# Feed-forward in pairs, free choice of PSUM banks, weights in ten pieces: a linear-attention and FFN kernel on one core

## The chip, the cores and the metric

The kernel runs on 1 core of one Trainium2 chip. The metric is the device time of one execution in microseconds (us). "Span" is the part of it that the profile covers, about 1 to 2 us less. The engines are TensorE (PE in the profile; its weight loads are PEld), VectorE (DVE), ScalarE (ACT), GpSimd (POOL) and SyncE (SP, which only issues transfers here). Each engine works through its own list of instructions in the order in which the program was built, and waits by semaphores for the others.

## The reference

```python
# B=4, H=8, S=768, D=48; FFN 384 -> 2048 -> 384 over 3072 tokens
for t in range(S):
    cur = einsum('bhd,bhe->bhde', u[None] * kt, vt)
    y[:, :, t] = einsum('bhd,bhde->bhe', rt, state + cur)
    state = w[None, :, :, None] * state + einsum('bhd,bhe->bhde', kt, vt)
x = y.transpose(0, 2, 1, 3).reshape(B * S, H * D)
return maximum(x @ w_in, 0) ** 2 @ w_out
```

The kernel cuts time into 6 chunks of 128 steps. A chunk of one batch is a *unit*; there are 24 of them, and a unit is also one block of 128 rows of the FFN.

## The kernel before

The program lists small operations with their engines, estimated durations and dependencies. A greedy scheduler in Python then puts them in order while the program is built. So the order of every engine is fixed at build time, by modelled times. Per unit: load k, r, v; multiply by powers of w (`kw`, `rw`); `rk`, `rku`, `du`, `dv` for the u term; transposes and attention matmuls on TensorE (`trk`, `trr`, `am`, `ym`, `yt`) with two masks, `sm` and `yb` on DVE in between. The FFN follows for groups of units:

```python
ps_ring("a", 3); ps_ring("h", 3); ps_ring("o", 2)          # fixed shares of the 8 PSUM banks
...
nc.sync.dma_start(out=wb, in_=bass.AP(tensor=w.tensor, offset=w.offset, ap=[[0, 128], [1, HD]]))  # ahead of the first k
...
groups = [[0, 1], [2, 3]] + [list(range(i, i + B)) for i in range(B, NU, B)]   # two pairs, then fours
W_IN_AT, W_OUT_AT = (0, 0, 1, 1), (3, 3, 4, 4)             # w_in in 4 parts at units 0, 0, 1, 1; w_out at 3, 3, 4, 4
...
for us in groups:
    L = len(us)
    for f in range(NF):                                     # 16 blocks of 128 hidden columns
        def m1(e, ...):
            t = ps_tile(h, [128, L * C], F32)               # 512 columns for a four, 256 for a pair
            for kk in range(NK):
                nc.tensor.matmul(out=t, lhsT=w_in_sb[:, kk, f * 128 : (f + 1) * 128], rhs=xt..., ...)
        # relu on DVE or ACT, square on ACT or POOL, both on [128, L * C]
    for j, n in enumerate(us):
        for part in range(PARTS):                           # m2: 4 matmuls of w_out at a time
            ...
```

## Time and profile before

| | before |
|---|---|
| time, median of the first runs | 202.22 us (201.72 to 204.4) |
| span | 201.1 us |
| TensorE, DVE, ACT, POOL busy | 90%, 67%, 64%, 67% |
| first transposes of unit 0 | 9.8 us |
| first FFN matmul | 24.7 us |
| FFN of the first four units done | 64.0 us |
| last weights landed | 52.2 us |
| last matmul started | 197.1 us |

The page's 40 slices (5 us each) of the kernel before show the regimes. A digit is the busy share of that slice in tenths; PEclk is the clock granted to TensorE.

```profile
PE   7474798696699799999999999999999999999992
DVE  5896868279976787896988558887476564555200
POOL 2665918279969999999998999989984010422200
PEclk9976559999999999999999999999999999999999
DMA  4999999947349999848555649210011001111122
```

TensorE is full from slice 14 (70 us; slices are counted from 0) on, and holes fill the time before. The sums by windows of 10 us of the same kernel follow; after the window and its length come PE, PEld, DVE, ACT and POOL busy (number of instructions), the granted clock, the share of the transfer engines and GB/s.

```profile
10.00:20.00 10.00, 6.16 (x62) 3.94 (x61) 7.89 (x12) 3.87 (x6) 6.20 (x7) 0.67 1.10 188
20.00:30.00 10.00, 8.63 (x67) 6.16 (x65) 7.20 (x15) 5.11 (x11) 5.56 (x8) 0.50 1.12 194
50.00:60.00 10.00, 7.96 (x85) 4.92 (x84) 8.85 (x14) 5.08 (x9) 8.29 (x8) 1.00 0.39 77
```

Busy PE includes matmuls on zeros that are only meant to keep its clock up ("fillers"), so busy is not work. The chain of waits of the kernel before, in order of time (start, length, what), names the holes:

```profile
9.18 8.82 DMA rt<-in_r_dram
...
30.70 8.73 DMA w_out_sb<-in_moe_w_out_dram
...
50.29 1.27 DVE rp_74 L256
...
62.14 0.96 POOL kp_79 L253
63.09 1.27 POOL rp_76 L256
```

A load beside w_in, then w_out, then DVE and POOL that prepare units 4 to 7 one operation after another. The first group of four cannot start its FFN before all its four units are prepared.

One number is used: *useful work*. It is the sum, over TensorE's matmuls without fillers that started before a time t, of the spacing that each costs at full clock. The spacing is taken from the Trainium skill, "TensorE: Matmul & The Clock Gate", Back-to-back issue gap (columns/2.4 + 2.5 ns for a warm TensorE; the section calls it the gap of an isolated matmul, and gives about 131 ns each for a stream of 512-column ones). The formula holds in rows too: 9 matmuls of 512 columns in 1.94 us before, 216 ns each. The float32 matmuls of the start are left out. In all it is 161.3 us before, and it shows how far TensorE has come at a given time.

### The profile page before, as it was taken

The numbers are of one execution on the slowest core, as the hardware profiler recorded it, in microseconds if no ns is written. First come the engines' busy times: TensorE is split into PE (matmuls) and PEld (weight loads), VectorE is DVE, ScalarE is ACT, GpSimd is POOL, SyncE is SP. The second block draws the span as 40 slices with busy tenths as digits, with TensorE's granted clock in tenths as the row PEclk, the third lists the DMA queues.
The fourth block names the chain that finished last, engine by engine and source line by source line (L and its number), as shares of the span: only waits on it lengthen the run. The fifth ranks groups of instructions, "written<-read, shape, count | busy, mean of one in ns | idle before, by whom it ended". The sixth has DMA issues, their size and how long they took to land.

```text
span 201.1 us, 4167 instructions
## 1 busy us (share of the span) xinstructions
PE 180.6 (90%) x1565; PEld 108.8 (54%) x1565; DVE 134.0 (67%) x239; ACT 128.7 (64%) x243; POOL 135.2 (67%) x155
## 2 busy tenths in 40 slices
PE   7474798696699799999999999999999999999992
PEld 2143476474356446565565665566556655555551
DVE  5896868279976787896988558887476564555200
ACT  3533458468366488899978979876687755444211
POOL 2665918279969999999998999989984010422200
PEclk9976559999999999999999999999999999999999
DMA  4999999947349999848555649210011001111122
GB/s 108 199 173 204 181 209 131 209 81 110 50 105 255 210 179 213 176 86 199 119 117 118 158 83 203 73 39 18 26 42 39 35 7 39 41 39 42 39 78 78
DMA packets 82368, 22.68 MB, mean 113 GB/s; under 512 B 75436, under 2 KB 82348, under 8 KB 82348
## 3 DMA queue, kind: packets, MB, share of 16 engines
q1 hardware_dynamic: 78480, 19.08, 43.6%
q0 software_dynamic: 3712, 3.15, 10.3%
q10 hardware_dynamic: 156, 0.20, 0.4%
q8 instruction: 12, 0.20, 0.4%
q14 instruction: 8, 0.07, 0.1%
HBM read 20.84 MB, written 4.72 MB: 127 GB/s over the span
## 4 chain that ended last, share of the span: by engine, by line
PE 70%; DMA 9%; DVE 7%; POOL 5%; SPq 4%; issue 2%; ACT 1%; POOLq 0%; DVEq 0%; ACTq 0%
PE ps_h L396 28%; PE ps_o L429 28%; DMA rt<-in_r_dram 4%; PE ps_a L274 4%; DMA w_out_sb<-in_moe_w_out_dram 4%; SPq L241 4%; PE ps_a L321 3%; PE ps_a L364 2%; PE ps_a L346 2%; PE ps_a L341 2%; DVE AT L331 2%; PE ps_a L291 1%; POOL rk L247 1%; DVE rku L250 1%; POOL rku L250 1%
## 5 line engine op out<-in xcount | busy, mean ns | idle before, releaser
L407 DVE TENSOR_SCALAR gr<-ps_h 128x512 f32<-128x512 f32 (+1 forms) x84 | 51.7, 624 | 35.8 <-PE ps_h L396 30.9
L396 PEld LDWEIGHTS <-w_in_sb 128*128 128x128 bf16 x336 | 31.6, 100 | 20.6 <-issue 0.6
L331 DVE TENSOR_TENSOR AT<-ps_a,smask 128x512 bf16<-128x512 f32 x48 | 30.8, 682 | 3.8 <-PE ps_a L321 3.7
L247 POOL TENSOR_TENSOR rk<-rt,kt 128x384 f32<-128x384 f32 x24 | 25.4, 1062 | 6.0 <-DVE wsq L203 3.9
L280 ACT COPY rkT<-ps_a 128x1024 bf16<-128x1024 bf16 x24 | 24.3, 1011 | 4.7 <-PE ps_a L274 4.5
L250 POOL TENSOR_TENSOR rku<-rk,ub 128x384 f32<-128x384 f32 x20 | 20.2, 1008 | 0.3
L264 POOL TENSOR_TENSOR dv<-vb,du 128x384 f32<-128x384 bf16 x21 | 17.6, 840 | 3.9 <-DVE du L261 3.0
L409 ACT ACTIVATE gr<-ps_h 128x512 f32<-128x512 f32 (+1 forms) x28 | 13.8, 502 | 9.6 <-PE ps_h L396 9.2
L416 POOL TENSOR_TENSOR g_2869<-gr 128x512 bf16<-128x512 f32 x5 | 5.2, 1039 | 20.6 <-DVE gr L407 20.6
L437 ACT COPY osb<-ps_o 128x384 f32<-128x384 f32 x24 | 11.4, 476 | 11.3 <-PE ps_o L429 11.3
L259 ACT CAST vb<-vt 128x384 bf16<-128x384 f32 x24 | 12.1, 509 | 7.7 <-DMA vt<-in_v_dram 7.7
L354 DVE TENSOR_TENSOR yb<-ps_a,dv 128x384 bf16<-128x384 f32 x24 | 13.2, 550 | 4.6 <-PE ps_a L346 4.5
L261 DVE TENSOR_REDUCE du<-rku 128x8 f32<-128x384 f32 x24 | 13.1, 544 | 1.8 <-POOL rku L250 1.5
L149 PE MATMUL ps_a<-zb 128*128 128x512 bf16 (+1 forms) x28 | 10.6, 503 | 2.8 <-DVE zb L144 1.3
L429 PE MATMUL ps_o<-w_out_sb,g_2038 128*128 128x384 bf16 x64 | 13.0, 326 | 0.0
L429 PE MATMUL ps_o<-w_out_sb,g_1578 128*128 128x384 bf16 x64 | 12.9, 326 | 0.0
L429 PE MATMUL ps_o<-w_out_sb,g_2501 128*128 128x384 bf16 x64 | 12.9, 326 | 0.0
L396 PE MATMUL ps_h<-xt_2120,w_in_sb 128*128 128x512 bf16 x48 | 12.8, 379 | 0.0
L396 PE MATMUL ps_h<-xt_2624,w_in_sb 128*128 128x512 bf16 x48 | 12.8, 379 | 0.0
L429 PE MATMUL ps_o<-w_out_sb,g_1150 128*128 128x384 bf16 x64 | 12.7, 326 | 0.0
L396 PE MATMUL ps_h<-xt_1681,w_in_sb 128*128 128x512 bf16 x48 | 12.7, 379 | 0.0
L414 ACT ACTIVATE g_2501<-gr 128x512 bf16<-128x512 f32 x15 | 9.5, 633 | 4.8 <-DVE gr L407 4.6
(182 smaller groups left out, 394.5 us busy)
## 6 DMA issues: line engine op xcount, KB each, us to landing
kt<-in_k_dram SPq DMA_DIRECT2D x24, 192.0 KB, 3.6
rt<-in_r_dram SPq DMA_DIRECT2D x24, 192.0 KB, 4.1
vt<-in_v_dram SPq DMA_DIRECT2D x24, 192.0 KB, 4.0
out_dram<-osb SPq DMA_DIRECT2D x24, 192.0 KB, 2.1
w_in_sb<-in_moe_w_in_dram POOLq DMA_DIRECT2D x4, 384.0 KB, 7.7
w_out_sb<-in_moe_w_out_dram POOLq DMA_DIRECT2D x4, 384.0 KB, 6.0
wb<-in_w_dram SPq DMA_DIRECT2D x1, 192.0 KB, 3.8
ub<-in_u_dram ACTq DMA_DIRECT2D x1, 192.0 KB, 3.9
```

The source lines that it names most:

```text
L247: two(lambda e, T=T: e.tensor_tensor(T("rk"), T("rt"), T("kt"), ALU.mult)),
L250: two(lambda e, T=T: e.tensor_tensor(T("rku"), T("rk"), ub, ALU.mult)),
L259: lambda e, T=T: nc.scalar.copy(T("vb"), T("vt")), takes=[bufs["vb"]], uses=[bufs["vt"]])
L261: lambda e, T=T: nc.vector.tensor_reduce(T("du"), T("rku"), axis=mybir.AxisListType.X, op=ALU.add),
L264: two(lambda e, T=T: e.tensor_tensor(T("dv"), T("vb"), T("du")[:, :, None].to_broadcast([C, H, D]), ALU.mult)),
L280: lambda e, T=T, rk_p=rk_p: nc.scalar.copy(T("rkT"), rk_p.tile),
L331: lambda e, T=T, i=i, x=x: nc.vector.tensor_tensor(T("AT")[:, i], x.tile, smask[:, None, :].to_broadcast([128, NP, C]), ALU.mult),
L354: lambda e, T=T, y_p=y_p: nc.vector.tensor_tensor(T("yb"), y_p.tile.rearrange("t p i d -> t (p i d)"), T("dv").rearrange("t h d -> t (h d) ...
L396: nc.tensor.matmul(out=t, lhsT=w_in_sb[:, kk, f * 128 : (f + 1) * 128], rhs=xt.tile[:, kk].rearrange("p b t -> p (b t)"), start=(kk == 0), ...
L407: nc.vector.tensor_scalar(gr.tile[:, : L * C], h.tile, 0.0, None, ALU.max)
L409: nc.scalar.activation(gr.tile[:, : L * C], h.tile, AF.Relu)
L429: nc.tensor.matmul(out=o_p.tile, lhsT=g.tile[:, f, j, :], rhs=w_out_sb[:, f, :], start=(f == 0), stop=(f == NF - 1),)
```

## The change

Its intent is to let FFN start sooner and to fill the first 70 us:

```diff
-    groups = [[0, 1], [2, 3]] + [list(range(i, i + B)) for i in range(B, NU, B)]
+    for j in range(NU // L):                       # L = 2: pairs throughout
+        us = [units[L * j], units[L * j + 1]]
...
+        for f in range(NH):                        # NH = 8; two row blocks of h in one bank
+            def m1(...):
+                for z in range(2):
+                    for kk in range(NK):
+                        nc.tensor.matmul(out=psv(h, 2, L * C)[:, z],
+                            lhsT=w_in_sb[:, kk, (2 * f + z) * 128 : (2 * f + z + 1) * 128], ...)
...
-    ps_ring("a", 3); ps_ring("h", 3); ps_ring("o", 2)
+    limits = {"a": 4, "h": 3, "o": 4}              # any free bank, up to a limit per use
...
-    W_IN_AT, W_OUT_AT = (0, 0, 1, 1), (3, 3, 4, 4)
+    PIECES = (0, 1, 2, 4, 6, 8)                    # five pieces of w_in, five of w_out, in turn
+    w_ops.append(weights(i, which, w_ops[-3] if len(w_ops) >= 3 else units[2]["vt"]))
+    load(n, nm, w_ops[-3] if n == 4 and nm == "kt" else None)   # unit 4's k waits for weights
...
-    nc.sync.dma_start(out=wb, ...)                 # w over 128 partitions, 192 KB; u likewise
+    nc.tensor.matmul(out=psv(wb_p, H, D), lhsT=ones, rhs=wrow[:, :, :D], ...)   # float32, from 1.5 KB
+    nc.tensor.matmul(out=psv(ub_p, HD), lhsT=ones, rhs=urow, ...)
```

Further: six buffers for loads instead of five, three for x and g, `rkT`, `xt` and `osb` copies on ACT or DVE, DVE's help for the first six units instead of eight, measured durations in the scheduler's model, w^128 by Ln and Exp instead of seven squarings.

## The prediction

> What bounds it now. In the page's slices TensorE is full from 70 us to 197 us, with holes before. Start to start in the timeline, at full clock: three 128x512 matmuls of w_in take 0.65 us, four 128x384 of w_out 0.65 us, one unit's attention about 1.5 us. A unit (24 in all) costs 5.2 + 1.5 = 6.7 us, all together 161 us (estimate from these). The span is 201.1: some 36 us are start, holes and low clock (0.67 and 0.50 in 10 to 30 us), 3.6 us follow the last matmul.
>
> The holes, by the chain of waits up to 75 us: no transposes until 9.8 us (wb, 192 KB, before the first k; two table loads; seven squarings of wc); 9.2 to 18.0 an r load competing with w_in; 30.7 to 39.4 w_out; 42 to 69 DVE and POOL preparing four units while TensorE has little FFN. At 70 us four units' FFN is done.
>
> What changes. (1) Pairs throughout: xt of two units releases FFN, so most of the third hole (units 4 to 7) goes. w_in matmuls are 256 wide and double in number. The trace has some: nine to twelve in a row take 0.110 to 0.117 us each, against 0.108 for half of a 512-wide one; the change costs 1 to 4 us. The Trainium skill, "TensorE: Matmul & The Clock Gate", Back-to-back issue gap, gives N/2.4 + 2.5 ns, 109 ns, which agrees. Relu and square stay 128x512 (0.62, 0.63 us), so DVE, ACT and POOL work per unit hardly changes (about 16.6 of 20.2 us). (2) Free bank choice: 1 to 3 us of PSUM waits. (3) wb and ub (384 KB) become 3 KB and float32 matmuls; one activation table: transposes at about 7 instead of 9.8 us. (4) Weights wait for unit 2's v, three pieces in flight; unit 4's k waits for weights. Transfers stay the limit at first: DMA share is 1.1 in 10 to 40 us. By the queue table k, r, v cost about 3.2 us per unit, all weights 20.7 us of sixteen engines (estimates from its shares). "DMA: Bandwidth & Descriptors", Specifications, names 512 B as minimum for line rate; 75,436 of 82,368 packets are smaller, which stays. Four units, the weights and parts of two more divided by 1.1 give 37 us: FFN of pairs 0 and 1 runs as pieces land, from about 17 us, ending about 41; pair 2 starts about 45, after a small hole.
>
> Sum: from 45 us remain 20 units' FFN (104 to 107 us), 18 units' attention (27), the last chain (1 to 2) and 3.6: span 181, time about 182 us. Range 175 to 192. Faster by over 2%: 0.94; within 2%: 0.05; slower: 0.01.
>
> What would show it: real transposes near 7 us; w_in's first FFN matmul before 20 us (24.7 now); last weights landing at 35 to 43 us; TensorE tenths of 9 from slice 9 or 10; four units' FFN done by 45 us; 256-wide w_in matmuls spaced 0.109 to 0.117 us; POOL no longer at 100%.
>
> What would make it wrong: an instruction order made for weights that land sooner than they do, TensorE standing behind a piece with other work ready; low clock to 40 us, as fillers end early; DVE or ACT late for attention; POOL and DVE slowing one another (DVE multiplications of 0.55 us take up to 1.35).

## The result

| | before | after |
|---|---|---|
| time, median | 201.97 us (201.5 to 204.4, 4 runs) | 191.87 us (190.73 to 193.31, 4 runs) |
| ratio to before | | 0.951 (0.945 to 0.957) |
| span of the profiled run | 201.1 us | 190.1 us |
| first transposes of unit 0 | 9.8 us | 12.6 us |
| first FFN matmul | 24.7 us | 22.8 us |
| FFN of the first four units done | 64.0 us | 52.5 us |
| last weights landed | 52.2 us | 40.0 us |
| useful work at 30, 45, 70 us | 6.5, 18.2, 34.5 us | 8.1, 22.7, 46.0 us |

Ratios here and below are the mean time of one kernel's fast runs over that of the other's of the same rounds, so not quite the ratio of the medians that are quoted. A later set gave the changed kernel 191.43 us (190.07 to 193.43; one of the six is slow, the fast ones end at 192.2), ratio 0.949 (0.945 to 0.954). Its executions scatter by 2 to 3 us, which matters for what follows.

The gain is 10 us, where 20 were expected. The slices of the changed kernel (4.75 us each):

```profile
PE   6998868999979999999999999999999999999991
DVE  6199997679888778787687697778796765755741
POOL 3399553139999999999999999999997850440000
PEclk9999999999999999999999999999999999999998
DMA  6999499998799858948958684020020020110202
```

By its digits TensorE is full from slice 7 (33 us) on, with one hole at slice 11. DVE shows 9 in slices 2 to 5. The windows of the changed kernel, columns as above:

```profile
10.00:20.00 10.00, 9.22 (x85) 5.25 (x85) 9.82 (x15) 5.47 (x10) 8.60 (x9) 1.00 1.14 186
20.00:30.00 10.00, 7.02 (x76) 4.06 (x75) 9.86 (x18) 5.92 (x12) 5.78 (x7) 1.00 0.80 107
50.00:60.00 10.00, 8.65 (x110) 6.69 (x108) 8.57 (x17) 6.52 (x12) 9.98 (x12) 1.00 0.85 182
```

DVE has 9.8 us of work in each of the windows from 10 to 30 us; transfers fall to 107 GB/s in the second. The chain of waits of the changed kernel:

```profile
5.74 1.57 PE bank L303 x2
7.32 1.28 PE bank L313 x2
8.60 1.50 PE bank L307 x8
10.10 2.67 PE bank L282 x6
12.77 0.43 PE bank L437 x4
...
22.95 1.03 DVE rp L289
...
24.90 1.15 DVE rk L289
26.05 0.47 DVE dv L289
...
29.81 0.57 DVE yb L508
30.38 0.05 issue
30.42 0.34 PE bank L516 x3
30.76 2.62 PE bank L543 x24
```

L303, L313 and L307 are the float32 matmuls for w, u and w^128; L282 are six fillers; L437 are unit 0's transposes. How long these take differs between executions: up to 14 us the fillers of this trace lie 0.43 us apart, from 20 us on 0.22 us, so TensorE ran at half its later rate at the start, although the PEclk row shows 9 there. A second trace of the same kernel has unit 0's transposes at 9.6 us, and five other runs below with the same start have them at 9.4 to 9.5 us. So some 3 of the 12.6 us belong to this execution. From 15 to 30 us the chain runs almost wholly on DVE, which prepares units 0 to 3 and also does `rp`, `rk` and `dv`, work that POOL could take. The first 12 matmuls of w_in ran at 22.8 and 24.5 us. L516 is unit 3's transpose at 30.4 us, and only behind it in TensorE's order stand the next 24 (L543), which are pair 0's and need nothing of unit 3. POOL's own list in that time (start, length, engine, line, what; in brackets its idle time before and who ended it):

```profile
21.37 0.99 POOL L289 TENSOR_TENSOR rku<-rk,ub 128x384 f32<-128x384 f32 x1 [2.74 <-DVE rk L289]
22.31 0.76 POOL L380 DMA_DIRECT2D w_out_sb<-in_moe_w_out_dram  x1
...
29.27 0.78 POOL L380 DMA_DIRECT2D w_out_sb<-in_moe_w_out_dram  x1 [2.35 <-DMA w_in_sb<-in_moe_w_in_dram]
...
40.94 1.30 POOL L289 TENSOR_TENSOR kp<-kt,wk 128x384 bf16<-128x384 f32 x1 [6.47 <-DMA kt<-in_k_dram]
```

POOL stands behind DVE's `rk` while the fourth weight piece waits for POOL to issue it; then, after one `rp` at 24.6 us, it stands behind landing pieces and does no multiplications that would relieve DVE until 40.9 us. So three suspects share the first 41 us: the start on TensorE (L303 to L282), the landing of pieces and of unit 4's k (40.8 us), and DVE's preparation of units 0 to 3.

### The profile page after: what moved, and what is told of

Its sections match the earlier page's. It is cut to its first block, busy times and chain, and to the rows that moved or that the text cites. A ratio compares the mean times of both kernels' runs of the same rounds, so it can differ in the third digit from the quotient of the medians.

```text
span 190.1 us, 4626 instructions
## 1 busy us (share of the span) xinstructions
PE 179.0 (94%) x1807; PEld 130.8 (69%) x1807; DVE 139.9 (74%) x239; ACT 122.5 (64%) x212; POOL 134.1 (71%) x149
## 2 busy tenths in 40 slices
DMA packets 82504, 22.32 MB, mean 117 GB/s; under 512 B 75441, under 2 KB 82482, under 8 KB 82482
## 4 chain that ended last, share of the span: by engine, by line
PE 88%; DVE 8%; ACT 1%; issue 1%; DVEq 0%
PE bank L572 33%; PE bank L543 33%; PE bank L437 5%; PE bank L476 4%; PE bank L282 4%; DVE AT L484 2%; PE bank L500 2%; PE bank L516 2%; PE bank L495 2%; PE bank L451 2%; DVE yb L508 1%; ACT rkT L294 1%; DVE dv L289 1%; PE bank L303 1%; PE bank L307 1%
## 5 line engine op out<-in xcount | busy, mean ns | idle before, releaser
L572 PE MATMUL bank<-w_out_sb,g 128*128 128x384 bf16 x384 | 81.1, 326 | 0.1
L543 PE MATMUL bank<-xt,w_in_sb 128*128 128x256 bf16 x576 | 77.4, 272 | 0.6 <-ACT xt L294 0.6
L563 ACT ACTIVATE g<-gr 128x512 bf16<-128x512 f32 x86 | 54.1, 631 | 20.2 <-DVE gr L555 18.7
L555 DVE TENSOR_SCALAR gr<-bank 128x512 f32<-128x512 f32 x68 | 46.6, 691 | 26.9 <-PE bank L543 22.5
L543 PEld LDWEIGHTS <-w_in_sb 128*128 128x128 bf16 x576 | 54.4, 98 | 12.6 <-issue 0.7
L572 PEld LDWEIGHTS <-g 128*128 128x128 bf16 x384 | 34.1, 98 | 14.0 <-ACT g L563 0.6
L484 DVE TENSOR_TENSOR AT<-bank,smask 128x512 bf16<-128x512 f32 x48 | 30.8, 683 | 1.1 <-PE bank L476 0.8
L289 POOL TENSOR_TENSOR kp<-kt,wk 128x384 bf16<-128x384 f32 x23 | 23.9, 1043 | 10.7 <-DMA kt<-in_k_dram 6.5
L294 ACT COPY rkT<-bank 128x1024 bf16<-128x1024 bf16 x20 | 20.2, 1009 | 10.0 <-PE bank L437 9.7
L289 POOL TENSOR_TENSOR rku<-rk,ub 128x384 f32<-128x384 f32 x21 | 21.4, 1020 | 2.8 <-DVE rk L289 2.7
L289 POOL TENSOR_TENSOR rp<-rt,wr 128x384 bf16<-128x384 f32 x21 | 21.8, 1037 | 0.0
L294 ACT COPY xt<-bank 128x384 bf16<-128x384 bf16 x19 | 9.1, 479 | 13.7 <-PE bank L516 12.5
L282 PE MATMUL bank<-zb 128*128 128x512 bf16 x27 | 11.1, 529 | 1.7 <-DVE zb L269 1.7
```

Of the source, the lines that this page charges most:

```text
L282: nc.tensor.matmul(out=banks[7], lhsT=zb[:, :128], rhs=zb, start=True, stop=True, skip_group_check=True)
L289: return lambda e: NOW[e].tensor_tensor(dst(), a(), b_(), f)
L294: nc.scalar.copy(dst(), src())
L484: lambda e, T=T, i=i, x=x: nc.vector.tensor_tensor(T("AT")[:, i], psv(x, NP, C), smask[:, None, :].to_broadcast([128, NP, C]), ALU.mult),
L543: nc.tensor.matmul(out=psv(h, 2, L * C)[:, z], lhsT=w_in_sb[:, kk, (2 * f + z) * 128 : (2 * f + z + 1) * 128], rhs=XT()[:, kk].rearrange(" ...
L555: nc.vector.tensor_scalar(dst, src, 0.0, None, ALU.max)
```

## The experiments

All were run with the kernel before on the same chip in the same rounds; the five sets used three chips. Four theories are named in the expectations: *start* (TensorE's first transposes come late, or attention's preparation on DVE holds TensorE), *weights* (the landing of pieces and of unit 4's k paces it), and for two parts of the change the worth that the prediction gave them.

### Pairs alone, in the kernel before

```diff
-    groups = [[0, 1], [2, 3]] + [list(range(i, i + B)) for i in range(B, NU, B)]
+    groups = [[i, i + 1] for i in range(0, NU, 2)]       # and two row blocks of h per bank, 3 buffers of xt and g
```

> The kernel before with one thing changed: FFN in pairs throughout, two row blocks of h per bank, so relu and square stay 128x512; start, weights, banks as before. Prediction: most of the hole from 42 to 69 us goes, so 8 to 13 us of the gain come from this alone: 189 to 194 us. If the hole was due to the late loads and weights instead, or is only moved, it stays above 198.

193.62 us (193.47 to 193.82), ratio 0.964 (0.957 to 0.970). Pairs alone bring 3.7% of the 4.9 to 5.1% that the whole change brings, about three quarters. Useful work at 70 us is 44.3 us, against 34.5 before and 46.0 after. That part of the prediction held. (The edit also gives xt and g a third buffer and the scheduler new durations for relu, square and the matmuls.) All the rest of the change together is worth about 2 us.

### Banks divided as before

```diff
-    limits = {"a": 4, "h": 3, "o": 4}
+    limits = {"a": 3, "h": 3, "o": 2}      # and FIXED = {"a": (0, 1, 2), "h": (3, 4, 5), "o": (6, 7)} in the choice
```

> The changed kernel with the banks divided as before (three for attention, three for h, two for outputs) instead of free choice. Prediction: 1 to 3 us slower, 193 to 195. If the free choice does nothing: within 0.5 us. Neither start nor weights theory depends on it.

190.54 us (190.15 to 190.63), ratio 0.948 (0.942 to 0.954). The free choice is worth nothing in the changed kernel. The order that the scheduler makes differs in the two, so this measures choice and order together.

### The start: fillers, and float32 spreading

```diff
-        if o.by == "T" and o.gap > 0 and o.start < WARM_UNTIL:
+        if o.by == "T" and o.gap > 0 and 10.0 < o.start < WARM_UNTIL:
```

> The changed kernel without the six filler matmuls that stand in TensorE's line between the spreading of w and u and unit 0's transposes (2.7 us in the trace); everything else and all orders as they are. Start theory (the 4 us by which the first transposes are late are carried to the end): transposes start at 11.2 us at the latest instead of 12.6 (DVE delivers r's scaled copy at 11.25), and the time falls by 1 to 2.5 us, to 189.4 to 190.9. Weights theory (FFN before 41 us is paced by the landing pieces, whatever the start does): within 0.5 us of the changed kernel. If the six fillers are what keeps the clock up, it dips to 0.5 within 10 to 20 us and the time does not fall.

193.15 us (192.13 to 193.79), ratio 0.960 (0.955 to 0.966). Transposes start at 9.1 us and nothing is gained. PEclk by slices of this run:

```profile
PEclk9955996999999999999999999999999999999998
```

The clock is low in slices 2 and 3, and again in slice 6 (29 to 34 us), where TensorE has FFN: 8.1 us of useful work are done between 30 and 40 us, against 9.6 in the changed kernel. So this run does not test the start. Nor does it show that the missing fillers caused the dips, for with the fillers in place the trace of the divided banks has 5 in slice 3 too.

```diff
-        nc.tensor.matmul(out=psv(wb_p, H, D), lhsT=ones, rhs=wrow[:, :, :D], ...)
+        pass        # wb by nc.scalar.dma_start(out=wb, in_=bass.AP(..., ap=[[0, 128], [1, HD]])); ub likewise
```

> The changed kernel with w and u again spread over the partitions by transfers (two of 192 KB on ACT's queue, at the same place), not by float32 matmuls; same order of all other instructions. My prediction says that the float32 spreading saved 3 us, so this should be 2 to 3 us slower, 194 to 195. Start theory says the opposite: the three float32 groups hold TensorE from 5.7 to 10.1 us, two of them go (2.9 us), so transposes start 1 to 2.9 us earlier and the time falls by 1 to 2.5 us, to 189.4 to 190.9; the 384 KB cost less than 2 us of transfers. Weights theory: 0 to 2 us slower, for the added bytes.

192.05 us (189.5 to 193.31), ratio 0.948 (0.937 to 0.959). Three of its six runs are slow; the fast ones took 189.5 to 191.54 us. Transposes start at 10.0 us instead of 12.6, the rest of the order is the same, and the time stays the same within its scatter. So my 3 us for the float32 spreading are not right. The start theory in its first form (late transposes are carried to the end) is worth 1 us at most: the traced spans are 189.1 and 190.1 us, useful work at 30 us 9.7 and 8.1. What became of the 2.6 us the chain of waits of this run shows. Unit 3's transposes move from 30.4 to 27.9 us, and from 14.6 to 40.2 us the chain now runs on weight pieces and unit 4's k, not on DVE:

```profile
22.14 6.46 DMA w_in_sb<-in_moe_w_in_dram
28.60 0.29 issue
28.89 6.22 DMA w_out_sb<-in_moe_w_out_dram
```

The 24 matmuls of w_in start at 28.65 us, when their piece has landed. So with all bytes the pieces bind as soon as unit 3 is 2 us earlier. In this run unit 4's k landed at 40.2 us and the hole at 50 to 60 us stayed (8.65 of 10 busy, as in the changed kernel).

### The changed kernel again

> The changed kernel unaltered, as the reference of the three others on this chip: 190.5 to 193.5 us. (By the lengths of TensorE's matmuls in its first trace, 161.9 us of useful work in all, 8.1 us of it done at 30 us, 17.7 at 40, 27.7 at 50, 46 at 70.)

191.43 us (190.07 to 193.43), as expected.

### Weight pieces: five in flight, or behind fewer loads

```diff
-  w_ops[-3] if len(w_ops) >= 3 else units[2]["vt"]
+  w_ops[-5] if len(w_ops) >= 5 else units[2]["vt"]
```

> The changed kernel with five weight pieces allowed in flight instead of three, so POOL issues the first five back to back at about 15 to 19 us and no piece waits behind POOL's wait for DVE (17.4 to 22.3 us in the trace, when transfers fell to 64 GB/s). Weights theory (pieces and unit 4's k land late because the transfers idle 20 to 25 us): rates stay near 180 GB/s there, the last piece and unit 4's k land 2 to 4 us earlier, and the time falls by 2 to 4 us, to 188 to 190. Start theory (attention of units 0 to 3 on DVE, TensorE stands behind it until 30.4 us): no change within 1 us, or slower, as POOL's own work is held up.

188.75 us (188.22 to 189.0), ratio 0.937 (0.933 to 0.940): 2.7 us faster than the changed kernel, and with 0.8 us of scatter instead of 3. The last piece lands at 35.8 instead of 40.0 us, unit 4's k at 37.6 instead of 40.8. The slices of this run:

```profile
PE   6949899999999999999999999999999999999991
DMA  6999999959779929939985486020020010110202
```

The hole at slice 11 is gone, and so is the dip of transfers at slice 4. This agrees with the weights theory, but the order of the engines changed with it: 12 of the 24 matmuls of w_in now stand ahead of unit 3's transposes and start at 27.0 instead of 30.8 us. Landing and order are not separated here.

```diff
-  load(n, nm, w_ops[-3] if n == 4 and nm == "kt" else None)
+  load(n, nm, w_ops[-3] if n in (4, 5) else None)
```

> The changed kernel with all of units 4 and 5's loads behind the weights, not only unit 4's k (r and v of both go ahead of the first piece now, about 4 us of transfers). Weights theory: first pieces land about 4 us earlier, FFN of pair 0 does more before 30 us, but units 4 and 5 are ready later: useful TensorE work at 30 us rises from 8.1 to 10 to 12 us, the hole at 50 to 55 us grows; net -2 to +2 us. Start theory: work at 30 us does not change (within 1 us) and the time is the same or longer, for the later units alone.

192.46 us (191.83 to 194.19), ratio 0.957 (0.952 to 0.961). Useful work at 30 us is 9.6 instead of 8.1 us, at 55 us 31.1 in both. The time is within the range given for the weights theory; the work at 30 us is just short of its 10 to 12, and the hole at 50 to 55 us did not grow (3.5 us of work in it, 3.4 in the changed kernel). It tells little.

### All weights first

```diff
+    for i in range(4):      # before anything else; w, u and the first k wait for their landing
+        first.append(nc.gpsimd.dma_start(out=w_in_sb[:, :, fs], ...))
+        first.append(nc.gpsimd.dma_start(out=w_out_sb[:, ks, :], ...))
-    WARM0 = 9
+    WARM0 = 90              # fillers meanwhile
```

> The changed kernel with the weights' wait taken away: all weights land before the first k, w and u are loaded (these wait for them; fillers keep TensorE's clock up meanwhile), and the order is made for weights that are there. The time as such is longer, by some 20 us. What counts is the span from the first k load's issue to the end: 189.4 us in the changed kernel. Weights theory: it falls by 6 us or more, to 183 or less, for FFN of pair 0 then runs while units 2 and 3 are prepared. Start theory (attention's preparation holds TensorE): it falls by less than 3 us.

202.51 us (202.0 to 204.97), longer as it must be. The first k is issued at 20.4 us and the span ends at 200.2, so 179.8 us lie between, against 189.4 us in the changed kernel: 9.6 us less. The chain of waits of this run shows pair 0's FFN starting as soon as unit 1 is through, at 38.9 us, 18.5 us after the first k's issue:

```profile
37.72 0.34 PE bank L528 x3
...
38.90 2.62 PE bank L555 x24
```

In the changed kernel pair 0's first 12 matmuls start 22.1 us after the first k's issue, and the 24 that stand behind unit 3 30.0 us after it. Here unit 3 is hardly sooner (its `yb` ends 27.1 us after the first k's issue, 29.7 in the changed kernel), but no FFN of pair 0 stands behind it. By its size the predicted span of 181 us is that of a kernel whose weights are there; that may be chance, for five things go at once here: the landing of pieces, POOL's time to issue them, the order in which FFN stands behind unit 3, loads of k, r and v without weights beside them, and the start (behind 90 fillers unit 0's transposes come 6.9 us after the first k's issue, 11.8 in the changed kernel).

### Combining, and how far it goes

> Five weight pieces in flight and w, u spread by transfers, together. Alone they took the ratio to before to 0.937 and 0.948 (changed kernel 0.949 to 0.951). If the start matters once the pieces land earlier: ratio 0.925 to 0.932, about 187 us. If only the pieces' landing matters, whatever the start does: 0.934 to 0.939, as with five in flight alone.

188.9 us (188.17 to 189.53), ratio 0.937 (0.932 to 0.941): the start does not matter with earlier pieces either.

> As the former, but all ten pieces issued back to back by POOL as soon as unit 2's v has landed. Weights theory: transfers never idle before 40 us, unit 4's k lands earlier still, 0.5 to 2 us faster than with five. Against it: POOL does none of its own work for 8 us, so DVE carries attention of units 2 and 3 alone; if that weighs more it is 0.5 to 2 us slower.

188.02 us (187.77 to 188.47), ratio 0.933 (0.928 to 0.937). This was the fastest correct version that I ran: 14 us faster than before and 3.4 to 3.9 us faster than the changed kernel. Its edit is the one of five in flight with `units[2]["vt"]` as the only gate, plus w and u by transfers.

> As the first, but weights start after unit 1's v, one unit earlier. Weights theory in its simple form (earlier weights are better): useful TensorE work at 30 us grows by 1 us or more and the time falls by 1 to 2 us. If what binds is the sum of all transfers needed for the first six units and the weights, it only shifts the wait to units 2 and 3: within 1 us or slower.

189.02 us (188.38 to 190.84), ratio 0.938 (0.933 to 0.943): starting the weights one unit earlier gains nothing; later loads then land later (unit 3's v at 18.8 instead of 15.8 us, unit 4's at 27.7 instead of 17.7).

> Five weight pieces in flight and unit 4's k not held behind the weights, w and u as in the changed kernel. In the trace with five in flight POOL still waits 6.9 us for unit 4's k, which lands at 37.6 us, but TensorE has no hole after it. So: within 0.7 us of 188.75 (ratio 0.934 to 0.940). If unit 4's k does bind, it falls by 1 us or more.

189.97 us (189.82 to 190.62), ratio 0.942 (0.938 to 0.947), which is slower, outside the range given: unit 4's k ahead of the weights, with the order made for that, costs more than it brings.

> The version with ten pieces in flight and w, u by transfers, with the banks divided 3, 3 and 2 as before. In the changed kernel this division was 1 us faster than the free choice, not slower. If that was more than chance: 187 to 187.7 us. If the free choice has a worth once weights land earlier: 188.5 us or more.

190.04 us (189.18 to 190.59), ratio 0.948 (0.942 to 0.955). Here the divided banks cost 2 us against 188.02, where in the changed kernel they cost nothing. As both change the whole order, I do not put a worth on the free choice as such.

### Bytes or preparation

```diff
-  sl = slice(lo * 256, hi * 256) if which == "in" else slice(lo * 2, hi * 2)
+  sl = slice(lo * 256, lo * 256 + (hi - lo) * 128) if which == "in" else slice(lo * 2, lo * 2 + hi - lo)
   # FFN uses each loaded block twice: blk(2 * f + z) in place of 2 * f + z
```

> Wrong result on purpose: the changed kernel with half of the weights' bytes; each piece loads half of its columns (rows of w_out), and FFN uses each loaded block twice. Every instruction, its size and its place is the same; only the transfers are shorter (by half of the 11.9% of sixteen engines over 190 us that the weights' queue took, so about 11 us of transfers). If the sum of transfers up to unit 4's k (40.8 us) binds: unit 4's k lands 5 us or more earlier, the hole at 52 to 55 us goes, and the time falls by 3 to 6 us, to 185.5 to 188.5. If DVE's preparation of units 0 to 3 binds (9.8 of 10 us busy from 10 to 30 us): within 1 us of 191.5.

Wrong result, as intended. 191.53 us (190.77 to 193.34), ratio 0.959 (0.951 to 0.966). The instructions of all five engines stand in the same order as in the changed kernel. The third piece of w_in lands at 26.1 instead of 29.0 us, the last piece at 33.2 instead of 40.0, unit 4's k at 34.2 instead of 40.8, and the time does not move. The weights theory, in the form that the sum of transfers alone binds, falls. The chain of waits of this run shows why:

```profile
28.72 0.57 DVE yb L512
29.29 0.04 issue
29.34 0.34 PE bank L520 x3
29.68 2.62 PE bank L547 x24
```

The 24 matmuls still stand behind unit 3's transposes, and these behind DVE.

> Wrong result on purpose: half of the weights' bytes in the same way, in the version with ten pieces in flight and w, u by transfers (188.0 us). If transfers still bind there: 2 to 5 us faster, 183 to 186. If what is left is preparation of attention on DVE and POOL: within 1 us of 188.

187.16 us (186.64 to 188.42), ratio 0.936 (0.929 to 0.943) against 188.02 and 0.933: nothing.

```diff
+    gone = {f"{nm}{n}" for nm in ("rku", "du", "dv") for n in range(4)}   # on top of half bytes; dv is zero
     for o in placed:
+        if o.name in gone:
+            continue
```

> Wrong result on purpose: half of the weights' bytes, as before, and also no rku, du and dv for units 0 to 3 (about 2 us of DVE's and POOL's work per unit; POOL then also has no wait on DVE before its fourth piece). Halving the bytes alone did nothing (191.5 us): TensorE waited for unit 3's yb until 29.3 us, as with full bytes. Two-limits theory (pieces landing at 29.0 and DVE's preparation done at 30.4 us bind at the same moment, so lifting one shows nothing): unit 3's transposes move to 25 to 27 us, useful TensorE work at 30 us rises from 8.8 to 11 or more, and the time falls by 2.5 to 5 us, to 186.5 to 189. If the order of the engines holds it back elsewhere (hole at 51 to 53.6 us, units 4 and 5): less than 1.5 us.

185.99 us (185.62 to 188.73), ratio 0.922 (0.917 to 0.928): 5.5 us less than with half bytes alone by the medians, 4.7 us by the traced spans. (The two ran on different chips, where the kernel before took 201.8 and 202.55 us.) TensorE's order is the same as in the changed kernel. DVE lost 11 instructions of the first 30 us, which took 7.5 us in the run with half bytes. The chain of waits of this run, where the same places now stand 5 us earlier:

```profile
24.47 0.34 PE bank L522 x3
24.81 2.62 PE bank L549 x24
```

Useful work at 30 us is 13.7 us, against 8.8 with half bytes alone and 8.1 in the changed kernel. So DVE's preparation binds, and the pieces stand close behind it: with full bytes the third piece lands at 29.0 us, so FFN could not have moved much ahead of that. The edit also takes away POOL's wait on DVE's `rk`, which brings the fourth piece's issue from 21.4 to 18.7 us. Less work on DVE with the full bytes was not run. The run with w and u by transfers comes near to it: with unit 3 ready 2.5 us earlier and all bytes, TensorE waited for the pieces, and 1.0 us of span was won.

> Wrong result on purpose: ten pieces in flight with half of the bytes, and the order now made for pieces that take half of the time. Halving the bytes under the old order gave 187.2 against 188.0 us. If the order is what hid the gain: 183 to 186. If DVE's preparation binds: within 1 us of 187.

186.71 us (186.47 to 187.82), ratio 0.927 (0.922 to 0.932): 0.5 us below the same bytes under the old order by the medians. By this the order hides little. (The ratios, 0.927 and 0.936, are of different chips; they would allow 2 us.)

> The same order, made for pieces that take half of the time, with the full bytes (right result). If the order does most: 185 to 187. If TensorE then stands in line behind pieces that are not there yet (they land at 26.5 us and later): slower than 188.0, up to 190.

190.1 us (189.44 to 190.71), ratio 0.943 (0.937 to 0.947): with full bytes an order made for pieces that come sooner than they do costs 2 us. TensorE then stands behind pieces with other work ready.

Useful work at a few times sums it up (us, from the traces; "all weights first" is counted from 19.7 us on, by which its first k is issued later, its span too):

| | 30 us | 45 us | 55 us | 70 us | span of that trace |
|---|---|---|---|---|---|
| before | 6.5 | 18.2 | 23.8 | 34.5 | 201.1 |
| pairs alone | 7.9 | 19.9 | 29.7 | 44.3 | 191.7 |
| changed | 8.1 | 22.7 | 31.1 | 46.0 | 190.1 |
| w, u by transfers | 9.7 | 23.7 | 32.1 | 47.0 | 189.1 |
| five in flight | 10.2 | 24.3 | 34.2 | 49.2 | 187.2 |
| ten in flight, w, u by transfers | 10.4 | 24.6 | 34.6 | 49.6 | 186.5 |
| half bytes | 8.8 | 23.8 | 32.1 | 47.1 | 189.0 |
| half bytes, less DVE work | 13.7 | 28.5 | 36.8 | 51.9 | 184.3 |
| all weights first | 15.7 | 30.8 | 40.7 | 55.6 | 180.5 |

From 70 us on all of them run at full rate: span and work at 70 us add up to 235.6 to 236.4 us in every row. So what is missing at 70 us is missing at the end.

## Why the prediction was right or wrong

The direction was right, the size was not: 182 us were predicted, 191.4 to 191.9 measured, half of the gain.

- **Right: pairs.** "Most of the third hole goes" held. Pairs alone give about three quarters of the gain, and useful work at 70 us rises by 10 us in the kernel before.
- **Right: 256-wide matmuls.** They are spaced 109 ns, as given. With this spacing 240 more matmuls make 0.6 us in all, less than the 1 to 4 us given.
- **Right: last weights.** They land at 40.0 us, inside 35 to 43.
- **Wrong, the step that failed:** "FFN of pairs 0 and 1 runs as pieces land, from about 17 us, and ends about 41; pair 2 starts about 45." Measured: 22.8, 52.5 and 54.7 us. The sum took 131 to 134 us of work as left at 45 us, so 28 to 31 done; 22.7 were done, 5 to 8 us fewer. Another 2 us went in the hole at 52.4 to 54.7 us, where the chain names ACT's `rkT` and `xt` for units 4 and 5. That is the 9 us between 181 and 190.1 us of span, to within 2 us. I had set only the transfers against TensorE. In their place DVE's preparation of units 0 to 3 binds until 30.4 us (9.8 of 10 us busy for 20 us), because 24 matmuls of pair 0 stand behind unit 3 in TensorE's order, and the third w_in piece lands just before, at 29.0. The two limits are so close that a start 2.6 us earlier was enough to put the pieces on the chain. Lifting the bytes alone gave nothing, lifting both gave 5.5 us, and taking away landing, issue, order, competing transfers and part of the start together gave 9.6 us.
- **Why I missed it:** I used the steady average, 16.6 of 20.2 us of DVE, ACT and POOL per unit. Between 20 and 40 us POOL is not there to take its share: it does 2 us of work of its own in all, and otherwise issues pieces, or waits for them and for DVE. The Trainium skill, "Perfetto Trace Analysis", Optimization Strategy, says that a kernel can have several regimes in which the most-contended engine changes. This trace agrees: DVE from 10 to 30 us, TensorE afterwards.
- **Wrong: the start.** Transposes came at 12.6 us, not 7. In TensorE's line stood the float32 matmuls (1.57, 1.28 and 1.50 us) and six fillers (2.67 us), all at half of TensorE's later rate in this execution; in others with the same start transposes came at 9.4 to 9.6 us, still late. It cost 1 us at most: so much shorter was the traced span with transposes at 10.0 us, and with five pieces in flight nothing was won.
- **Wrong: banks** at 1 to 3 us. Nothing in the changed kernel (2 us in the version with ten pieces in flight).
- **Wrong: POOL no longer at 100%.** It stays at 9.7 to 10 of 10 from 60 to 140 us, and TensorE is full all the same.
- **A sign that misled:** "TensorE tenths of 9 from slice 9 or 10" came true but for one slice while the time was 10 us off. Busy tenths do not show how much work is still left.
- **What would make it wrong** named DVE, POOL and the order; DVE was given too little weight. DVE and POOL do slow one another: the two `rp` that DVE does from 10 to 31 us take 1.23 us on average, against 0.55 us alone, while the masks, which read PSUM, stay at 0.68. The Trainium skill, "GPSIMD Engine Reference", Specifications, says that the SBUF interfaces are shared and that DVE instructions with two SBUF inputs contend; the trace agrees.

What stays open: what DVE's relief itself gives with the full bytes, how much of the gain with five and ten pieces in flight is the order's, and whether the whole 9.6 us can be had without loading the weights first.

## What to carry to other kernels

Cost the start of a kernel as its own regime, engine by engine, with the work that each engine is kept from doing; a sum per unit that fits on average says nothing about the first 30 us. When two limits end at nearly the same moment, lifting one shows nothing, so a null result clears a suspect only once the other is lifted too. Look at what an engine that issues transfers in order stands behind between two issues: letting all pieces go at once came out 3.4 us faster here, together with the order that the scheduler made for it. Which of the two gave it is not shown; in the old order pieces that landed 3 to 7 us earlier gave nothing.

## What the Trainium skill lacked or had wrong

- "TensorE: Matmul & The Clock Gate" gives no spacing for float32 operands. Here a 384-column float32 matmul with one contraction row appears as two matmuls and took 1.57 and 1.28 us in the profile's chain, and four 1-column ones appear as eight and took 1.50 us; in the run with all weights first, behind 90 fillers, the same three took 0.84, 0.65 and 0.79 us. For 512-column matmuls back to back the page has two figures, about 131 ns under "Back-to-back issue gap" and 215.7 ns under "Wait — 56ns, not 53.3ns?"; 9 in a row took 216 ns each here.
- "GPSIMD Engine Reference", Specifications, names the contention for the SBUF interfaces without a size. Here a DVE multiplication of two 128x384 float32 inputs took 0.55 us alone and up to 1.36 us beside POOL, and POOL's own 0.99 us grew to at most 1.32 in the changed kernel.
- "DMA: Bandwidth & Descriptors" gives no rate for a mix of small and large packets. Here, with 75,441 of 82,504 packets under 512 B, the rate stood at 151 to 220 GB/s in the changed kernel's slices with a DMA digit of 9; what the packet size alone costs was not measured.
